# Delta rule and top-2 router on one core: keys used as they come, block copies laid out contiguously, joins and router pieces moved in the program

## The chip, the cores and the metric

One core of a Trainium2 chip runs the whole program in one launch. The metric is device time in microseconds (us), the median of the runs; lower is better.

## What is computed

For each of 4 x 8 batch-head pairs the delta rule walks 768 tokens with a 48 x 48 state. Its output, as 3072 tokens of 384 numbers, goes through a noisy top-2 router into 8 experts (384 to 1024 to 384).

```python
k_n = k / (np.linalg.norm(k, axis=-1, keepdims=True) + 1e-06)
for t in range(S):
    y[:, :, t] = np.einsum('bhd,bhde->bhe', q[:, :, t], state)
    v_old = np.einsum('bhde,bhd->bhe', state, kt)
    state = state + bt[:, :, :, None] * np.einsum('bhd,bhe->bhde', kt, vt - v_old)
# x: (B*S, H*D)
noisy_logits = x @ w_gate + np.log1p(np.exp(x @ w_noise)) * noise
# two largest per token, softmax over the two, then
out[token] += weight * (np.maximum(x @ w1[e], 0.0) @ w2[e])
```

## The kernel before, in words

The delta rule is done in 12 chunks of 64 tokens. A **unit** is one chunk of two batch entries: 128 partitions hold 2 x 64 tokens, the free axis 8 heads. A chunk has two units, and two chunks (four units) make a **step**; there are six steps. Everything is float32.

Per unit: `products` (L313) transposes the keys on TensorE (`turned`, L293, matmuls of L297, copied to `kT` on ScalarE), forms K K^T in `p_k` (L307), and copies its 32 x 32 blocks on ScalarE: the diagonal blocks to `gd` (L330, four copies of 32 partitions), the off-diagonal ones to `at` (L332, two copies of 32 partitions). Per step, `normalize` (L261) comes first: ScalarE squares the keys, VectorE sums them, a chain of small operations gives the inverse norm `ksc`, and GpSimd multiplies the keys by it (L287), so that every later use of the keys waits for that.

Per step, `invert` (L334) inverts the 32 x 32 triangles of all 128 (unit, head, block) cases at once on VectorE: a blockwise transposition of `gd` to `t` (L343), a product with `low_b`, 30 pairs of operations (L353, L357), a scaling, and two transpositions to `tt` (L369) and `tb` (L373). `join` (L377) copies `tt` into the 64 x 64 matrices `w64` on ScalarE (L387, four copies a unit), and fills their fourth quarter by two rounds of matmuls (L393, L402) with ScalarE copies between (L398, L407).

`recur` (L467) is the recurrence of a chunk in three stages: the state's part is subtracted from v (`p_b`, L307; VectorE L477), the rows are solved (`p_u`, L485; ScalarE copy `u`, L490), and the state is updated (`p_s`, L503; VectorE L510 or L512; GpSimd copies of it to `wide`, L515). `within` makes the masked products of queries and keys `qk` one chunk ahead, `answer` the outputs `y` and the router's logits one chunk behind. `route` (L518) handles the four tiles of a finished step on VectorE: top two, then the row of each token in its expert's list, by two matmuls into `p_at` (L583, L584), then eight GpSimd scatters to DRAM (`spread`, L170).

The program's loop hands out these pieces: `inverse`, `answers`, `nexts` are generators, and `take(work, n)` runs n pieces at the marked places. In an even chunk the inversion of the next step starts, and `normalize` and the route of the step before are there whole; the joins of the next step come at the end of an odd chunk. A scheduler then fixes one order per engine, which the engine follows strictly, so a waiting instruction holds all behind it. `gd`, `t`, `tt` and `tb` have one buffer each.

When all rows are scattered, the experts run one after the other on TensorE (L702, L709, L718), and a loop over the 24 tiles gathers and adds the two rows of each token (L783 to L798).

## Time and profile before

| | before |
|---|---|
| median of 3 runs | 1264.98 us (1264.11 to 1267.48) |
| the profiled execution, its own time | 1273.34 us |
| its span | 1271.6 us |
| TensorE matmul busy | 936.2 us (74%) |
| VectorE busy | 341.6 us (27%) |
| ScalarE busy | 332.5 us (26%) |
| GpSimd busy | 168.7 us (13%) |
| mean granted TensorE clock | 0.795 of full |

The shares are means over three stages that differ much: the delta rule and router (to about 588 us), the experts, and the last gather. A term is read from the timeline of its own stage. "issue" in a row is idle time before an instruction for which the profile shows no releaser.

### The profile page before, as it was taken

How to read it: one execution, taken by the hardware profiler on the slowest of the kernel's cores; microseconds unless marked ns; L12 is line 12 of the kernel's file. 1: busy time of each engine (PE TensorE's matmuls, PEld its weight loads, DVE VectorE, ACT ScalarE, POOL GpSimd, SP SyncE). 2: the span in 40 equal slices, each digit the busy share in tenths (PEclk: the TensorE clock that was granted, in tenths of full speed). 3: DMA queues.
4: the chain of work that ended last, by engine and by line, in shares of the span. 5: the costliest groups of instructions: out<-in, count | busy, mean ns of one | idle time of the engine just before them, and what ended most of it. 6: DMA issues, size and time to landing. Idle time of an engine off the chain costs nothing. (4 is left out here: it accounts for less than half of the span.)

```text
span 1271.6 us, 20241 instructions
## 1 busy us (share of the span) xinstructions
PE 936.2 (74%) x8634; PEld 628.1 (49%) x8634; DVE 341.6 (27%) x923; ACT 332.5 (26%) x693; POOL 168.7 (13%) x222
## 2 busy tenths in 40 slices
PE   2143756847648678834999999999999999999400
PEld 2133745736537567633565555555555555555200
DVE  2764382572753712121010010101101010110112
ACT  3474644554355233110202011020201102010021
POOL 5102113032131120220000000000000000000265
PEclk9555766657558655556999999999999999999755
DMA  5941292726622120116112231301213120100266
GB/s 105 343 144 19 54 324 74 209 83 186 228 64 40 27 63 3 51 44 236 52 42 93 75 112 62 124 34 54 100 74 112 62 81 0 38 7 23 86 199 186
DMA packets 142658, 124.31 MB, mean 98 GB/s; under 512 B 84704, under 2 KB 134880, under 8 KB 142560
## 3 DMA queue, kind: packets, MB, share of 16 engines
q1 hardware_dynamic: 135520, 103.95, 26.0%
q0 software_dynamic: 6144, 18.88, 4.7%
q8 instruction: 70, 1.15, 0.3%
q10 hardware_dynamic: 896, 0.10, 0.1%
q14 instruction: 28, 0.23, 0.1%
HBM read 59.99 MB, written 62.91 MB: 97 GB/s over the span
## 5 line engine op out<-in xcount | busy, mean ns | idle before, releaser
L709 PE MATMUL p_h<-xe,w1e 128*128 128x448 f32 x768 | 290.7, 540 | 1.5 <-DVE xe L703 1.5
L718 PE MATMUL p_o<-w2e,hT 128*128 128x384 f32 x896 | 290.3, 486 | 0.0
L718 PEld LDWEIGHTS p_o<-w2e,hT 128*128 128x128 f32 x896 | 170.2, 190 | 119.6 <-issue 3.0
L709 PEld LDWEIGHTS p_h<-xe,w1e 128*128 128x128 f32 x768 | 145.3, 190 | 142.9 <-issue 139.7
L713 ACT ACTIVATE hT<-p_h 128x448 f32<-128x448 f32 x128 | 69.6, 544 | 526.8 <-PE p_h L709 526.8
L722 DVE COPY yr<-p_o 128x384 f32<-128x384 f32 x56 | 31.2, 558 | 543.0 <-PE p_o L718 543.0
L783 POOL DMA_INDIRECT got<-rows_y,slot x48 | 46.9, 977 | 644.0 <-PEq L756 624.4
L297 PE MATMUL p_t<-ident,kp 128*128 128x128 f32 x96 | 22.6, 390 | 86.6 <-POOL kp L287 85.8
L353 DVE TENSOR_TENSOR part<-t 128x30 f32<-128x30 f32 (+9 forms) x180 | 64.1, 356 | 4.7
L357 DVE TENSOR_TENSOR t<-t,part 128x30 f32<-128x30 f32 (+9 forms) x180 | 63.8, 354 | 4.8
L330 ACT COPY gd<-p_k 32x256 f32<-32x256 f32 x96 | 56.3, 586 | 25.0 <-PE p_k L307 14.4
L387 ACT COPY w<-tt 32x256 f32<-32x256 f32 x96 | 60.1, 626 | 9.5 <-DVE tt L369 8.2
L297 PEld LDWEIGHTS p_t<-ident,kp 128*128 128x128 f32 x96 | 16.2, 203 | 88.6 <-POOL kp L287 86.8
L170 POOL DMA_INDIRECT rows_x<-y,slot x48 | 46.9, 976 | 85.9 <-issue 52.0
L515 POOL COPY wide<-st 64x384 f32<-64x384 f32 x44 | 26.3, 599 | 172.2 <-DVE st L512 136.2
L583 PE MATMUL p_at<-r_taken,mask_u 128*128 128x32 f32 x12 | 3.6, 396 | 54.4 <-DVE gate L531 22.7
L702 PE MATMUL p_xt<-ident,xr 128*128 128x128 f32 x168 | 21.7, 290 | 27.9 <-DMA xr<-rows_x 27.9
L503 PE MATMUL p_s<-u,kp 64*64 64x48 f32 x704 | 30.8, 284 | 15.2 <-issue 15.1
L440 PE MATMUL p_y<-u,qk 64*64 64x48 f32 x768 | 40.2, 274 | 0.0
L790 ACT ACTIVATE got<-got,gate 128x384 f32<-128x384 f32 x24 | 14.7, 614 | 97.2 <-DMA got<-rows_y,slot 91.1
L307 PE MATMUL p_b<-st,kT 64*64 64x48 f32 x704 | 31.2, 283 | 12.0 <-issue 11.9
L440 PEld LDWEIGHTS p_y<-u,qk 64*64 64x64 f32 x768 | 36.5, 189 | 4.5 <-issue 3.7
(119 smaller groups left out, 892.9 us busy)
## 6 DMA issues: line engine op xcount, KB each, us to landing
rows_y<-zero SPq DMA_DIRECT2D x8, 3264.0 KB
w1e<-in_moe_w_dram SPq DMA_DIRECT2D x8, 1536.0 KB
w2e<-in_moe_w_dram SPq DMA_DIRECT2D x8, 1536.0 KB
rows_x<-zero SPq DMA_DIRECT2D x8, 1344.0 KB
xr<-rows_x SPq DMA_DIRECT2D x8, 1344.0 KB
rows_y<-yr SPq DMA_DIRECT2D x56, 192.0 KB
kp<-in_k_dram SPq DMA_DIRECT2D x48, 96.0 KB
qp<-in_q_dram SPq DMA_DIRECT2D x48, 96.0 KB
```

The lines of the kernel that those rows point to most:

```text
L170: d = nc.gpsimd.indirect_dma_start(out=rows_x, out_offset=bass.IndirectOffsetOnAxis(ap=slot, axis=0), in_=rows, in_offset=None,).ins
L297: nc.tensor.transpose(p_t[:, j], src[:, 2 * j : 2 * j + 2], ident)
L307: nc.tensor.matmul(out[rows_of[b], z, j], lhsT[rows_of[z], j, rows_of[b]], rhs(rows_of[z], j, b), start=(j == 0), stop=(j == NP - 1), skip ...
L330: nc.scalar.copy(gd[rows], p_k[rows, :, :, n * Q : (n + 1) * Q])
L353: nc.vector.tensor_tensor(out=part, in0=t[:, j + 1 :, j, None].to_broadcast(shape), in1=t[:, None, j, 0:j].to_broadcast(shape), op=ALU.mult,)
L357: nc.vector.tensor_tensor(out=t[:, j + 1 :, 0:j], in0=t[:, j + 1 :, 0:j], in1=part, op=ALU.add)
L387: nc.scalar.copy(w64[rows, :, cols], tt[rows])
L440: nc.tensor.matmul(p_y[b, h], qk[b, h % 2, h // 2], u[b, h], start=(c == 0 and h == 0), stop=(h == H - 1), skip_group_check=True,)
L709: nc.tensor.matmul(p_h, w1e[:, do, fo * 128 : (fo + 1) * 128], xe[:, do, cols], start=(do == 0), stop=(do == KT - 1),)
L713: nc.scalar.activation(hT[:, fo, cols], p_h, ACTF.Relu)
L718: nc.tensor.matmul(p_o, hT[:, fo, i * 128 : (i + 1) * 128], w2e[:, fo], start=(fo == 0), stop=(fo == FT - 1),)
L783: nc.gpsimd.indirect_dma_start(out=g, out_offset=None, in_=rows_y, in_offset=bass.IndirectOffsetOnAxis(ap=slot[:, n : n + 1], axis=0),)
```

## The change

- `normalize` is gone: the keys stay as loaded. The squared norms are read from the diagonal of the transposed `gd` in `invert`, and the chain that gives the norm now stands there, on [128, 32] tiles, followed by d = beta / norm^2 and by `low_d`, a GpSimd product of 128 x 1024 numbers that the inversion's first product needs. `low_b`, which it replaces, depended on inputs alone.
- `norms`, transposed back, multiplies v on GpSimd: `scale(c)`, two products of 128 x 384 per chunk, as large as the products on keys that are gone.
- `gd` and `tt` are laid out [128, 32 heads, 32] instead of [128, 32, 32 heads], so that ScalarE's block copies read and write runs of 32; the VectorE transpositions of `gd` and to `tt` now have one strided side. `at` is copied once per unit with 128 partitions.
- At the start the joins of only two units come ahead of the loop. Later joins are given out in pieces, the first of them at the end of the odd chunk.
- `route` has yields, and is begun in the middle of the even chunk. Its running count is one reduction; the sum over earlier tiles goes to four matmuls with `ones` (there was one). Three small VectorE operations are fused away.
- On the load queue, the keys of step 2 now stand ahead of the eight clears of `rows_x`.

```diff
-        def normalize(s):
...
         def products(n):
...
-            for b in range(2):
-                for n in range(2):
-                    rows = slice(b * C + n * Q, b * C + (n + 1) * Q)
-                    nc.scalar.copy(gd[rows], p_k[rows, :, :, n * Q : (n + 1) * Q])
-                    if n == 0:
-                        nc.scalar.copy(at[rows], p_k[rows, :, :, Q:C])
+            nc.scalar.copy(at, p_k[:, :, :, Q:C])
+            for lo in range(0, 128, Q):
+                rows = slice(lo, lo + Q)
+                nc.scalar.copy(gd[rows], p_k[rows, :, :, lo % C : lo % C + Q])
 
         def invert(s):
...
+            nc.vector.transpose(
+                out=t, in_=step[s, "gd"].rearrange("p h i -> p i h"),
+            )
+            nc.vector.tensor_copy(ss, diagonal)
+            nc.vector.tensor_scalar_max(root, ss, 1e-30)
+            nc.scalar.activation(root, root, ACTF.Ln)
+            nc.scalar.activation(root, root, ACTF.Exp, scale=0.5)
+            yield
+            nc.vector.reciprocal(norm, root)
+            nc.vector.tensor_tensor(out=norm, in0=norm, in1=ss, op=ALU.mult)
+            nc.vector.tensor_tensor(out=norm, in0=norm, in1=root, op=ALU.add)
+            nc.vector.tensor_scalar(
+                out=norm, in0=norm, scalar1=0.5, scalar2=1e-6, op0=ALU.mult, op1=ALU.add
+            )
+            nc.vector.tensor_tensor(out=d, in0=norm, in1=norm, op=ALU.mult)
+            nc.vector.reciprocal(d, d)
+            nc.vector.tensor_tensor(out=d, in0=d, in1=beta_s, op=ALU.mult)
+            nc.gpsimd.tensor_tensor(
+                out=low_d, in0=low, in1=d[:, None, :].to_broadcast([128, Q, Q]), op=ALU.mult
+            )
+            nc.vector.transpose(out=norms, in_=norm)
+            yield
+            nc.vector.tensor_tensor(out=t, in0=t, in1=low_d, op=ALU.mult)
...
+            nc.vector.transpose(out=tt.rearrange("p h i -> p i h"), in_=scaled)
...
+        def scale(c):
+            for n in range(c * NU, (c + 1) * NU):
+                nc.gpsimd.tensor_tensor(
+                    out=v, in0=v,
+                    in1=step[s, "norms"][:, i * H : (i + 1) * H, None].to_broadcast(
+                        [128, H, D]
+                    ),
+                    op=ALU.mult,
+                )
...
         def route(s):
...
+            for i in range(1, US):
+                nc.tensor.matmul(
+                    p_at[:, i:], ones, taken[:, 0 : US - i],
+                    start=False, stop=False, skip_group_check=True,
+                )
+            nc.tensor.matmul(
+                p_at, ones, before[:, None, :].to_broadcast([128, US, E]),
+                start=False, stop=True,
+            )
...
         for c in range(NCH):
             s = c // 2
+            scale(c)
             if c % 2 == 0:
                 inverse = [invert(s + 1)] if s + 1 < NS else []
                 take(inverse, 1)
-                if s + 2 < NS:
-                    normalize(s + 2)
...
             for i, _ in enumerate(recur(c)):
                 if i == 0:
                     take(answers, 3)
                     if grams:
                         products(grams[0])
-                    take(inverse, 6)
+                    take(inverse, 9)
+                    take(joins, 2)
+                    take(routes, 3)
                 elif i == 1:
-                    take(answers, 3)
+                    take(answers, 4)
                     if grams:
                         products(grams[1])
-                    take(inverse, 6)
+                    if c % 2 == 0:
+                        take(inverse, 9)
+                        take(joins, 2)
+                        if c:
+                            routes = [route(s - 1)]
+                    else:
+                        take(inverse, 99)
+                    take(routes, 3)
```

How the instructions move, at three places. TensorE, where the first chunk's solve (`p_u`) stands, before: it follows the transposition of a key tile of step 2.

```order
L402 MATMUL p_x<-w_3_157,x 32x32 x16
L307 MATMUL p_q<-qT,kT 64x64 x16
L297 MATMUL p_t<-ident,qp_142 128x128 x4
L307 MATMUL p_q<-qT,kT 64x64 x16
L297 MATMUL p_t<-ident,kp_132 128x128 x4
L485 MATMUL p_u<-v,w_0_148 64x48 x7
```

The same place in the change:

```order
L384 MATMUL p_x<-w_0_148,x 32x32 x16
L384 MATMUL p_x<-w_1_151,x 32x32 x16
L267 MATMUL p_t<-ident,kp_132 128x128 x4
L375 MATMUL p_x<-tb,at 32x32 x16
L277 MATMUL p_k<-kT 64x64 x16
L375 MATMUL p_x<-tb,at 32x32 x2
L384 MATMUL p_x<-w_2_154,x 32x32 x16
L375 MATMUL p_x<-tb,at 32x32 x14
L480 MATMUL p_u<-v,w_0_148 64x48 x16
```

The solve now follows the joins of its own two units and parts of the other two; the key transposition ahead of it needs a load alone.

TensorE in a later step, before: the router's `p_at` stands behind the solve of the even chunk and ahead of its state update `p_s`.

```order
L485 MATMUL p_u<-v,w_3_157 64x48 x16
L451 MATMUL p_xt<-ident,y 128x128 x3
L459 MATMUL p_xt<-wgn,xT 128x16 x3
L583 MATMUL p_at<-r_taken,mask_u 128x32
L297 MATMUL p_t<-ident,kp_126 128x128 x4
L584 MATMUL p_at<-r_earlier,ones 128x32
L297 MATMUL p_t<-ident,qp_144 128x128
L307 MATMUL p_k<-kT 64x64 x16
L503 MATMUL p_s<-u,kp_132 64x48 x16
L503 MATMUL p_s<-u,kp_134 64x48 x16
```

In the change:

```order
L480 MATMUL p_u<-v,w_3_157 64x48 x16
L433 MATMUL p_xt<-ident,y 128x128 x3
L267 MATMUL p_t<-ident,kp_126 128x128 x4
L441 MATMUL p_xt<-wgn,xT 128x16 x3
L277 MATMUL p_k<-kT 64x64 x16
L498 MATMUL p_s<-u,kp_132 64x48 x16
L498 MATMUL p_s<-u,kp_134 64x48 x16
L267 MATMUL p_t<-ident,qp_144 128x128 x4
L267 MATMUL p_t<-ident,qp_146 128x128 x4
L277 MATMUL p_q<-qT,kT 64x64 x32
L277 MATMUL p_b<-st_2965,kT 64x48 x16
L277 MATMUL p_b<-st_2986,kT 64x48 x16
```

`p_at` follows these rows: it has moved behind the state update, the next queries and the next `p_b`.

VectorE at the turn of a step, in the change (before, a transposition of `gd` is followed by the product with `low_b` after one state update, and the two long transpositions to `tt` and `tb` stand half a step ahead):

```order
L350 TENSOR_TENSOR scaled<-t,d 128x1024
L355 STREAM_TRANSPOSE tt<-scaled 128x32x32
L356 STREAM_TRANSPOSE tb<-scaled 128x32x32
L507 TENSOR_TENSOR st_3375<-p_s,st_2965 128x384
L307 STREAM_TRANSPOSE t<-gd 128x1024
L507 TENSOR_TENSOR st_3396<-p_s,st_2986 128x384
L313 COPY ss<-t 128x32
L314 TENSOR_SCALAR root<-ss 128x32
L401 TENSOR_TENSOR qk<-p_q,mask 128x512
L318 RECIPROCAL norm<-root 128x32
L319 TENSOR_TENSOR norm<-norm,ss 128x32
```

The odd chunk's state update now stands directly behind the end of one inversion and around the start of the next.

## Rows read from the trace of the kernel before

**Rows 1.** Page, part 2: busy tenths and clock tenths, 31.8 us per digit.

```profile
PE   2143756847648678834999999999999999999400
...
PEclk9555766657558655556999999999999999999755
```

**Rows 2.** Timeline, 560 to 600 us: start us, us, engine, line, operation; idle before it.

```profile
571.01 0.96 POOL L170 DMA_INDIRECT rows_x<-y,slot  x1 [0.30 <-issue]
...
588.45 4.49 PE L702 MATMUL p_xt<-ident,xr 128*128 128x128 f32 x21 [27.93 <-DMA xr<-rows_x]
```

**Rows 3.** Groups by line: xcount | busy us, mean ns of one | idle before, releasers.

```profile
L297 PE MATMUL p_t<-ident,kp 128*128 128x128 f32 x96 | 22.6, 390 | 86.6 <-POOL kp L287 85.8 <-issue 0.8
...
L583 PE MATMUL p_at<-r_taken,mask_u 128*128 128x32 f32 x12 | 3.6, 396 | 54.4 <-DVE gate L531 22.7 <-DVE gate L601 22.5 <-DVE r_taken L531 9.2
```

**Rows 4.** Timeline, startup, 14 to 154 us.

```profile
14.48 0.94 ACT L270 ACTIVATE ksq<-kp 128x384 f32<-128x384 f32 x2
...
20.48 1.97 PE L297 MATMUL p_t<-ident,kp 128*128 128x128 f32 x8 [20.48 <-POOL kp L287]
...
36.03 0.58 ACT L330 COPY gd<-p_k 32x256 f32<-32x256 f32 x1
...
36.64 1.25 DVE L343 STREAM_TRANSPOSE t<-gd 128x1024 f32<-128x1024 f32 x1 [17.27 <-ACT gd L330]
...
54.25 2.06 PE L297 MATMUL p_t<-ident,kp 128*128 128x128 f32 x8 [22.42 <-POOL kp L287]
...
69.53 1.92 PE L393 MATMUL p_x<-tb,at 32*32 32x32 f32 x64 [3.78 <-DVE tb L373]
...
115.03 1.11 PE L297 MATMUL p_t<-ident,kp 128*128 128x128 f32 x4 [23.71 <-POOL kp L287]
...
116.08 0.98 PE L485 MATMUL p_u<-v,w 64*64 64x48 f32 x13
...
125.31 1.02 DVE L510 COPY st<-p_s 128x384 f32<-128x384 f32 x2 [11.30 <-PE p_s L503]
...
151.92 1.25 DVE L343 STREAM_TRANSPOSE t<-gd 128x1024 f32<-128x1024 f32 x1 [1.47 <-ACT gd L330]
```

**Rows 5.** Groups by line again: prices of ScalarE, GpSimd and VectorE operations.

```profile
L387 ACT COPY w<-tt 32x256 f32<-32x256 f32 x96 | 60.1, 626 | 9.5 <-DVE tt L369 8.2
...
L330 ACT COPY gd<-p_k 32x256 f32<-32x256 f32 x96 | 56.3, 586 | 25.0 <-PE p_k L307 14.4 <-remote 6.1 <-PE p_s L503 3.6
...
L332 ACT COPY at<-p_k 32x256 f32<-32x256 f32 x48 | 19.3, 401 | 0.0
...
L407 ACT COPY w<-p_x 32x256 f32<-32x256 f32 x48 | 17.4, 363 | 6.7 <-PE p_x L402 5.9
...
L338 POOL TENSOR_TENSOR low_b<-low,beta_b 128x1024 f32<-128x1024 f32 x6 | 14.1, 2357 | 28.3 <-DVE tb L373 11.2 <-DVE r_d L531 6.0 <-DVE r_a_hit L531 5.7
...
L373 DVE STREAM_TRANSPOSE tb<-scaled 128x1024 f32<-128x1024 f32 x6 | 12.0, 1993 | 0.0
...
L369 DVE STREAM_TRANSPOSE tt<-scaled 128x1024 f32<-128x1024 f32 x6 | 7.4, 1242 | 0.1
...
L278 DVE RECIPROCAL rec<-root 128x32 f32<-128x32 f32 x6 | 2.1, 347 | 1.1 <-ACT root L277 1.1
```

**Rows 6.** Timeline, one step, 253 to 288 us.

```profile
258.13 1.12 PE L297 MATMUL p_t<-ident,kp 128*128 128x128 f32 x4 [6.11 <-POOL kp L287]
...
264.08 0.86 ACT L490 COPY u<-p_u 128x384 f32<-128x384 f32 x2
...
278.70 0.61 PE L583 MATMUL p_at<-r_taken,mask_u 128*128 128x32 f32 x2 [11.38 <-DVE gate L531]
...
287.29 0.46 PE L503 MATMUL p_s<-u,kp 64*64 64x48 f32 x4 [0.95 <-issue]
```

**Rows 7.** Windows: us, busy of PE, PEld, DVE, ACT, POOL; granted clock; DMA share.

```profile
300.00:310.00 10.00, 7.36 (x185) 6.39 (x181) 1.11 (x2) 6.33 (x15) 0.00 (x0) 1.00 1.02 349
...
490.00:500.00 10.00, 10.00 (x132) 8.76 (x135) 0.00 (x0) 2.22 (x6) 0.00 (x0) 0.50 0.02 3
```

More of the change, by code (lines that the diff above doesn't have):

```diff
@@ L347, in invert @@
-            nc.vector.tensor_tensor(out=t, in0=t, in1=low_b, op=ALU.mult)
+                out=low_d, in0=low, in1=d[:, None, :].to_broadcast([128, Q, Q]), op=ALU.mult
+            )
+            norms = step[s, "norms"] = sb([128, UH], "norms", 2)
+            nc.vector.transpose(out=norms, in_=norm)
+            yield
+            nc.vector.tensor_tensor(out=t, in0=t, in1=low_d, op=ALU.mult)
             for j in range(1, Q - 1):
@@ L573, in route @@
             top1, hit1 = take_largest(rest, "b")
+            p1, den = gates[1][:, to], gates[0][:, to]
+            vv(p1, top1, top0, ALU.subtract)
+            nc.scalar.activation(p1, p1, ACTF.Exp)
             taken, at = full("taken"), full("at")
             vv(taken, hit0, hit1, ALU.add)
-            earlier = full("earlier")
-            for i in range(US):
-                nc.vector.tensor_copy(earlier[:, i], before)
-                vv(before, before, taken[:, i], ALU.add)
             p_at = bank([128, US, E], "p_at")
             nc.tensor.matmul(p_at, mask_u, taken, start=True, stop=False)
-            nc.tensor.matmul(p_at, ones, earlier, start=False, stop=True)
+            for i in range(1, US):
[6 more added lines that the diff above has]
+                start=False, stop=True,
+            )
+            yield
+            count = sb([128, E], "r_count", 1)
+            nc.vector.tensor_reduce(
+                out=count, in_=taken.rearrange("p u e -> p e u"), axis=AX.X, op=ALU.add
+            )
             vv(at, p_at, part[:, None, :].to_broadcast([128, US, E]), ALU.add)
+            vv(before, before, count, ALU.add)
             for hit, slot in ((hit0, slots[0]), (hit1, slots[1])):
@@ L608, in take, with now @@
                     work.pop(0)
+        def now(*work):
+            take(list(work), 999)
         nc.scalar.preload_act_table_set("natural_log_exp_and_others")
@@ L618, in deltanet @@
         load_router()
+        for n in range(2 * US, 3 * US):
+            load(n, "k")
         for e in range(E):
             cleared.append(clear(rows_x, e * N, e * N + TILES * 128))
-        for n in range(2 * US, 3 * US):
-            load(n, "k")
         first_weights = load_weights(w_even, 0)
-        def now(work):
-            for _ in work:
-                pass
-        normalize(0)
         for n in range(US):
@@ L632, in deltanet @@
         now(invert(0))
-        normalize(1)
         for n in range(US, 2 * US):
             products(n)
-        for n in range(US):
-            now(join(n))
         for n in range(NU):
             now(within(n))
-        def route_later(s):
-            route(s)
-            yield
-        inverse = []
+        for n in range(NU):
+            now(join(n))
+        inverse, joins, routes = [], [join(n) for n in range(NU, US)], []
         for c in range(NCH):
             s = c // 2
+            scale(c)
             if c % 2 == 0:
@@ L658, in deltanet @@
             nexts = [within(n) for n in range((c + 1) * NU, (c + 2) * NU) if n < NCH * NU]
-            joins = [join(n) for n in range((s + 1) * US, (s + 2) * US) if n < NS * US]
             for i, _ in enumerate(recur(c)):
@@ L679, in deltanet @@
                                 load(n, "k")
-        now(answer(NU * NCH - 2))
-        now(answer(NU * NCH - 1))
-        route(NS - 1)
+        now(*(answer(n) for n in range((NCH - 1) * NU, NCH * NU)))
+        now(route(NS - 1))
         return first_weights
```

96 lines of the change are left out of this document (33 added, 63 removed).

## The prediction, made before the change was run

> **What bounds the kernel now.** I read the page's slices first [rows 1]. In each slice the reader is to see which engine is full: TensorE stands between 1 and 8 tenths in the first 18 slices and at 9 from then to near the end. The kernel is thus two programs in a row: a delta rule with a router, in which no engine is full, and a dense stretch of experts. The border is sharp in the timeline [rows 2]: the last scatter of tokens starts at 571.01 us, the first expert matmul at 588.45, when the gathered rows have landed. From there on nothing is changed, so what the change is worth is how much earlier 588.45 comes.
>
> Second, the groups with their idle time [rows 3]. Two of them say what TensorE waits for in the first stage: 85.8 us for the keys that GpSimd has multiplied by their inverse norms, and 54.4 us for the router's counts, at `p_at`. Third, the timeline, to see where these waits lie and what is queued behind them. At the start [rows 4] the key transposition of 115.03 waited 23.71 us, and directly behind it stands the first solve, 116.08; the first state is there at 125.31. In a later step [rows 6] the transposition of 258.13 waited 6.11 us with the even chunk's solve behind it, and `p_at` of 278.70 waited 11.38 us with the state update behind it. Both are on the recurrence. I take them at full length, and look for what comes late next.
>
> **Term 1, the start.** Before, ScalarE's first piece of work is a square at 14.48, the transposition of keys starts at 20.48, ScalarE's last block copy at 36.03, and the first VectorE transposition at 36.64 [rows 4]. Now the keys need no norm. Per unit ScalarE has one copy to `kT` (0.59, as the wider copies of this trace) and five block copies. The block copies to `gd` and `w64` took 586 and 626 ns; those of the same size with both sides in runs took 401 (`at`) and 363 (`w64` from `p_x`) [rows 5]. The new ones lie between 363 and 626; I take 400, because the shape is that of `at`, and the same for the `at` copy over 128 partitions. Four units are 4 x (0.59 + 5 x 0.40) = 10.4 us, with about 1 us of matmuls ahead: the transposition of `gd` comes at about 26 in place of 36.64.
>
> The inversion gets longer. The transpositions of `gd` and to `tt` get a strided side; between 1.24 us (`tt` now) and 1.99 us (`tb`, strided on both) [rows 5] I take 1.99, which adds 1.5. The norm chain adds some nine small VectorE operations at 0.19 to 0.35, two on ScalarE and their handovers, an estimate of 3.4 us from the 347 ns of a reciprocal [rows 5] and the normalization's own like operations. `low_d` is 2.36 us on GpSimd, by `low_b`, and no longer ahead of time; at the start two products on v stand ahead of it, 1.8. Against this, the norms of step 1 no longer interrupt the first inversion (four sums and seven small operations, about 3.6). From 26, the 32.9 us from transposition to first join matmul (36.64 to 69.53) [rows 4] plus 1.5 + 3.4 + 4.2 - 3.6 give about 64; I say 66, for a queue of v products on GpSimd.
>
> Then the gain. Before, the first solve came 46.6 us after the first join, because all four joins and the key transposition of step 2 stood ahead, and those keys' norms stood behind the second inversion on VectorE. Now two joins and parts of two more stand ahead: two rounds of ScalarE copies and matmuls, about 11 us. The solve is at 77, the state some 10.5 later (9.2 before), at 87.5 in place of 125.31. The next chunk I let take as long as before: third transposition 26.6 us after the first state, 151.92. In the change the transpositions to `tt` and `tb`, 4 us, stand in that place on VectorE. So 118 in place of 152: **34 us**. Bounds: 20 (the joins' queue costs what the keys' did for one unit more) and 42.
>
> Of the other startup waits for keys, 20.48 is in this term, and the 22.42 at 54.25 [rows 4] cost nothing, since VectorE was in the inversion until about 69.
>
> **Term 2, keys in the later steps.** 85.8 less 20.48, 22.42 and 23.71 leaves 19.1 us in three waits. The next transposition needs only a load that was issued a step ahead; the solve behind it needs v and `w64`, which were there several us before. **19 us**; bounds 10 (something else late) and 19. GpSimd's products on v replace those on keys one for one and are needed a chunk later, so I price them at nothing; the cover is the rest of the chunk, and without it four products at 0.9 us a step would show.
>
> **Term 3, the route.** Of the 54.4 us, the sixth wait, about 5.5, lies behind the recurrence and stays. For the others `p_at` now stands behind the state update, the queries and `p_b`, some 6 us of TensorE work. VectorE, though, mixes route and inversion one for one: behind the state update I count in its order some 14 inversion operations, 15 of the route and four long ones ahead of the counts, about 11 us. So about 5 us of each wait stay; the first route, which stands whole behind the second loop inversion, keeps all. Gains of 6, 6, 4 and 1 make **17 us**; bounds 0 and 43. The three extra matmuls with `ones`, at the 0.4 of a `p_at` matmul [rows 3], are paid for by the eight small VectorE copies and sums between the two matmuls that go. The scatters stay eight a step, and with them a stretch in which TensorE goes on in bursts with 0.95 us of idle time, released by nothing that the profile shows [rows 6]; I gain and lose nothing there.
>
> **Term 4, ScalarE's queue.** In each chunk with new keys the copies to `u`, 264.08 in [rows 6], wait behind six block copies of 4 x 0.59 + 2 x 0.40 = 3.15 us, now 2.0. Eight chunks at 1.15: **9 us**, bounds 0 and 12. The shorter `w64` copies (16 a step) fall while TensorE is at other work: nothing.
>
> **Longer inversions in later steps** I price at nothing: `tb` was done about 40 us ahead of the joins that need it, and VectorE has to stay below the step's 84 us. If that cover goes, it is the rival below. Moving the keys ahead of the clears on the load queue shifts loads that were early: nothing.
>
> **Sum.** 34 + 19 + 17 + 9 = 79 us. The profiled execution took 1273.34 us with a span of 1271.6, 8.4 above the median of 1264.98; taken off the median, 79 gives **1186 us** (and a span near 1193). Ends of the terms do not come all together; its own range is 1160 to 1212.
>
> **Rival 1, the waits move.** Behind the keys and the counts stands the chain itself, and p_b, solve and update have to meet VectorE between inversion operations. If the later steps stay as long as they are, only term 1 is left: 1265 - 34 = 1231. For it: five later steps are alike although their waits differ, and VectorE's order now puts both state updates against long operations. Against: nothing else in the later steps ended TensorE's waits for long.
>
> [...]
>
> **Rival 3, slower: the inversion becomes the bound.** Its chain is now transposition, norm, ScalarE, GpSimd's `low_d` behind the copies of the state, then 60 operations mixed with the route, and the two transpositions directly ahead of the joins. Per step that is 1.5 + 3.4 + 2.4, about 8 us with handovers, and the lead of 40 us is given up by the new order. If `tb` ends later than the odd chunk's state update in every step, five steps give 5 x 8 = 40 and the removed waits bring nothing, since TensorE waits at the joins; with 10.6 gained at the start and two startup inversions of 8 each lost, this is +45: 1310. It decides from the point where VectorE's step passes 84 us. Against: VectorE was busy 341.6 us in the whole run.
>
> **Rival 4, no effect**: the start is bound elsewhere (the loads) and all else is hidden: about 1262.
>
> **How the numbers follow.** Forecast 0.62, rival 1 0.16, rival 2 0.13, rival 3 0.06, rival 4 0.03. Over or under 0.3%, about 4 us, is what a measurement can tell here: faster 0.91, same 0.03, slower 0.06. The range from 1142 to 1233 takes in most of rivals 1 and 2 and leaves out rivals 3 and 4 and the far ends, some 0.15.
>
> **What would show it.** First `gd` transposition near 26, first state near 88, third transposition near 118, first expert matmul near 510; no wait of the key transposition for GpSimd; `p_at` waits near 5 us; block copies near 0.40. It is wrong if the step from transposition to transposition stays at 84 (rival 1), if the clock row shows long stretches of 9 ahead of the experts (rival 2), or if the join matmuls of L375 wait for `tb` in the later steps (rival 3).

## The result, and the profile after

The change takes 1202.05 us (median of 4 runs, 1196.75 to 1207.17), the kernel before beside it 1266.23 (4 runs, 1264.11 to 1281.67): a ratio of 0.9468, 95% interval 0.9382 to 0.9554, so 64 us less. The forecast was 1186, the range 1142 to 1233.

The profiled execution of the change took 1196.75 us with a span of 1195.0. Against the span of 1271.6 before, that is 76.3 us, 12 more than the medians show: the profile of before lies 7 above its median, that of after 5 below. Everything changed lies ahead of the first expert matmul, which comes at 511.37 in place of 588.45 [rows 2]: 77.1 us. The page's slices of the change, for [rows 1], 29.9 us a digit:

```profile
PE   3265678788676788089999999999999999999200
...
PEclk9657566757666665589999999999999999999655
```

TensorE is fuller (5 to 8 from the third slice to the sixteenth, where it was 3 to 8), and its granted clock is hardly higher: a mean of 0.64 up to the first expert matmul, where it was 0.63. The start, for [rows 4], from the timeline of the change, VectorE first (start, length, engine, line, operation, idle time before it):

```profile
24.80 1.90 DVE L307 STREAM_TRANSPOSE t<-gd 128x1024 f32<-128x1024 f32 x1 [18.52 <-ACT gd L300]
...
87.13 0.56 DVE L505 COPY st<-p_s 128x384 f32<-128x384 f32 x1 [4.53 <-PE p_s L498]
...
109.28 1.92 DVE L307 STREAM_TRANSPOSE t<-gd 128x1024 f32<-128x1024 f32 x1
```

The same view of TensorE, first join, first solve, and what comes about the second chunk:

```profile
63.59 1.92 PE L375 MATMUL p_x<-tb,at 32*32 32x32 f32 x64 [22.61 <-DVE tb L356]
...
78.45 1.94 PE L480 MATMUL p_u<-v,w 64*64 64x48 f32 x32
...
115.02 1.14 PE L277 MATMUL p_q<-qT,kT 64*64 64x64 f32 x32 [11.09 <-ACT qT L269]
...
144.18 1.09 PE L480 MATMUL p_u<-v,w 64*64 64x48 f32 x14
153.05 1.13 PE L277 MATMUL p_k<-kT 64*64 64x64 f32 x32 [7.79 <-ACT kT L269]
153.96 2.97 PE L480 MATMUL p_u<-v,w 64*64 64x48 f32 x50
```

And the first expert matmul, for [rows 2]:

```profile
511.37 4.72 PE L714 MATMUL p_xt<-ident,xr 128*128 128x128 f32 x21 [27.90 <-DMA xr<-rows_x]
```

The first transposition of `gd` comes at 24.80 (26 was said), the first solve at 78.45 (77), the first state at 87.13 (87.5), the third transposition at 109.28 (118). Then TensorE waits for ScalarE: 11.09 us for `qT` at 115.02, and 7.79 us for `kT` at 153.05, in the middle of the solve of chunk 2. The groups that answer to [rows 3] and [rows 5]:

```profile
L369 ACT COPY w<-tt 32x256 f32<-32x256 f32 x96 | 38.6, 402 | 31.2 <-DVE tt L355 29.8
L300 ACT COPY gd<-p_k 32x256 f32<-32x256 f32 x96 | 34.8, 362 | 0.9
...
L328 POOL TENSOR_TENSOR low_d<-low,d 128x1024 f32<-128x1024 f32 x6 | 14.1, 2347 | 26.9 <-DVE d L326 23.9 <-DMA kp<-in_k_dram 2.9
...
L355 DVE STREAM_TRANSPOSE tt<-scaled 128x1024 f32<-128x1024 f32 x6 | 11.5, 1921 | 0.1
...
L297 ACT COPY at<-p_k 128x256 f32<-128x256 f32 x24 | 8.9, 372 | 11.7 <-PE p_k L277 11.5
...
L582 PE MATMUL p_at<-r_taken,mask_u 128*128 128x32 f32 x12 | 3.4, 369 | 20.5 <-DVE r_taken L526 15.0 <-DVE gate L526 5.5
```

The wait for GpSimd's products on the keys is gone; that at `p_at` fell from 54.4 to 20.5 us; the block copies take 362 and 402 ns where they took 586 and 626; a VectorE transposition with one strided side takes 1.92 us. What TensorE waits for now, in the list of waits up to the first expert matmul (total us, times, longest):

```profile
PE p_q L277 <- ACT qT L269: 23.7, 10, 11.1
...
PE p_k L277 <- ACT kT L269: 21.5, 6, 7.9
PE p_b L277 <- DVE qk L401: 15.1, 5, 5.1
...
PE p_u L480 <- ACT y L427: 8.1, 3, 3.4
```

Before, the same four were 6.8, 8.4, none and none. So by the first pair of traces the start and the later steps came out close to the sum. From the first solve of chunk 0 the gain is 37.6 us (116.08 to 78.45), from that of chunk 2 31.6 (175.75 to 144.18), and the rest of the stage takes 367.2 us in place of 412.7, 45.5 less where terms 2 to 4 add up to 45. The experiments show that it was made up of other things than those terms.

### The profile page after: what moved, and what is told of

The parts are those of the page before. It is cut to its first block, busy times and chain, and to the rows that moved or that the text cites. A ratio compares the mean times of both kernels' runs of the same rounds, so it can differ in the third digit from the quotient of the medians.

```text
span 1195.0 us, 20175 instructions
## 1 busy us (share of the span) xinstructions
PE 926.0 (77%) x8670; PEld 624.2 (52%) x8670; DVE 325.7 (27%) x875; ACT 272.5 (23%) x645; POOL 170.7 (14%) x222
## 5 line engine op out<-in xcount | busy, mean ns | idle before, releaser
L344 DVE TENSOR_TENSOR t<-t,part 128x30 f32<-128x30 f32 (+9 forms) x180 | 60.6, 337 | 4.7
L480 PE MATMUL p_u<-v,w 64*64 64x48 f32 x768 | 42.3, 281 | 9.3 <-ACT y L427 8.1
L510 POOL COPY wide<-st 64x384 f32<-64x384 f32 x44 | 23.5, 535 | 161.8 <-DVE st L507 145.7
L480 PEld LDWEIGHTS p_u<-v,w 64*64 64x64 f32 x768 | 40.0, 200 | 12.6 <-issue 9.7
L369 ACT COPY w<-tt 32x256 f32<-32x256 f32 x96 | 38.6, 402 | 31.2 <-DVE tt L355 29.8
L422 PE MATMUL p_y<-u,qk 64*64 64x48 f32 x768 | 45.0, 295 | 0.8 <-issue 0.8
L422 PEld LDWEIGHTS p_y<-u,qk 64*64 64x64 f32 x768 | 41.0, 209 | 5.2 <-issue 5.0
L375 PE MATMUL p_x<-tb,at 32*32 32x32 f32 x768 | 23.4, 229 | 24.4 <-DVE tb L356 22.6
L277 PE MATMUL p_b<-st,kT 64*64 64x48 f32 x704 | 25.8, 269 | 18.9 <-DVE qk L401 15.1
L277 PE MATMUL p_k<-kT 64*64 64x64 f32 x768 | 21.4, 266 | 21.5 <-ACT kT L269 21.5
L277 PE MATMUL p_q<-qT,kT 64*64 64x64 f32 x768 | 17.6, 248 | 24.6 <-ACT qT L269 23.7
```

What stands on the lines that cost most here:

```text
L277: nc.tensor.matmul(out[rows_of[b], z, j], lhsT[rows_of[z], j, rows_of[b]], rhs(rows_of[z], j, b), start=(j == 0), stop=(j == NP - 1), skip ...
L344: nc.vector.tensor_tensor(out=t[:, j + 1 :, 0:j], in0=t[:, j + 1 :, 0:j], in1=part, op=ALU.add)
L369: nc.scalar.copy(w64[rows, :, cols], tt[rows])
L422: nc.tensor.matmul(p_y[b, h], qk[b, h % 2, h // 2], u[b, h], start=(c == 0 and h == 0), stop=(h == H - 1), skip_group_check=True,)
L480: nc.tensor.matmul(p_u[b, h], w64[b, h], r[b, h], start=(h == 0), stop=(h == H - 1), skip_group_check=True,)
```

## The experiments

Kernels of one set ran on one chip, beside runs of the kernel before. The ratio is the one to before in the same set. "Later steps" is the stretch from the first solve of chunk 2 to the first expert matmul, in the one profiled execution; the busy and idle time of TensorE and its clock come from the windows view of that stretch. Executions of one kernel lie up to 23 us apart, so a difference of traces below 10 us is weak, and the ratios decide. The traces of e, b and d lie 13, 8 and 4 us above the medians of their kernels, that of i 8 below. Kernels c and d have the order of before, and d its layouts too, but both keep the change's rewritten count of the router.

| kernel | ratio, 95% interval | chunk 2 solved at | later steps | busy | idle | clock |
|---|---|---|---|---|---|---|
| before, first trace | | 175.75 | 412.7 | 260.7 | 152.0 | 0.61 |
| change, first trace | 0.9468 (0.938 to 0.955) | 144.18 | 367.2 | 253.7 | 113.5 | 0.63 |
| e: before again | | 180.30 | 360.9 | 230.4 | 130.5 | 0.66 |
| f: layouts alone | 0.9781 (0.970 to 0.986) | 163.60 | 342.1 | 222.3 | 119.8 | 0.68 |
| d: keys alone | 0.9979 (0.995 to 1.001) | 153.21 | 381.6 | 248.0 | 133.7 | 0.63 |
| c: keys, layouts, old order | 0.9650 (0.960 to 0.970) | 142.93 | 353.6 | 232.0 | 121.6 | 0.67 |
| b: keys, new order | 0.9937 (0.990 to 0.997) | 150.82 | 379.5 | 265.4 | 114.2 | 0.61 |
| a: the change again | 0.9657 (0.961 to 0.971) | 140.88 | 348.1 | 249.8 | 98.3 | 0.64 |
| h: the change, scatters left out | 0.9660 (0.960 to 0.972) | 144.21 | 337.7 | 237.1 | 100.6 | 0.68 |
| i: `w64` copies on GpSimd | 0.9495 (0.944 to 0.955) | 141.44 | 324.8 | 237.3 | 87.5 | 0.67 |
| j: `low_d` undone | 0.9618 (0.956 to 0.968) | 141.50 | 338.3 | 239.1 | 99.1 | 0.67 |
| l: i and j together | 0.9484 (0.942 to 0.954) | 138.95 | 322.1 | 230.6 | 91.5 | 0.70 |

"Chunk 2 solved at" is the first matmul of 64. In the change, a, b, h and j the first 14 stand 8 to 14 us ahead of the other 50 (a: 140.88 and 150.68), in the others of the table less than 2 us (c: 142.93 and 144.60). Counted from the 50, the change gains 23.5 us up to there in the first pair and 31.3 from e to a, and 8 us more behind it than the table says.

### a and e: both kernels once more

No edit.

> The change itself, timed again beside the three kernels that undo parts of it, so that all are compared on one chip. Theory 1 (the sum of the prediction, with waits traded against waits): 1202, a ratio to before of 0.947. Theory 2 (the profiled execution of the change, 1196.75, was a lucky one and that of before, 1273.34, an unlucky one): also 1202, with single executions spread over 10 us or more, while border times of one trace against another are no better than that.

Measured: 1170.96 us (6 runs) against 1213.5 (23 runs). Both theories said 1202, and both missed: in this set the change is 31 us faster than in the first, the kernel before 53 us, and the gain is 42 us, not 64. What is different in the kernel before?

> The kernel before, profiled once more, since its median was 1266 beside the first runs of the change and 1213.5 beside the four kernels of the first set. Theory 1 (what differs is how TensorE gets on beside the scatters): if this execution is near 1213, its state updates p_s run without the gaps of 0.25 to 0.97 us that the first trace shows beside the scatters (15.1 us of such idle time at p_s, 11.9 at p_b), and the steps are some 8 us shorter each, while the start is as it was; if it is near 1265, the gaps are there. Theory 2 (the granted clock differs): the gaps are the same and the clock of the first 590 us is higher than the 0.54 to 0.70 of the first trace.

Measured: 1221.96 us in one run; the runs of before beside it have a median of 1209.09 (17 runs), so this execution is 13 us above it. The two groups of the first trace, state updates and state parts:

```profile
L307 PE MATMUL p_b<-st,kT 64*64 64x48 f32 x704 | 31.2, 283 | 12.0 <-issue 11.9
L503 PE MATMUL p_s<-u,kp 64*64 64x48 f32 x704 | 30.8, 284 | 15.2 <-issue 15.1
```

and of this one:

```profile
L307 PE MATMUL p_b<-st,kT 64*64 64x48 f32 x704 | 24.1, 271 | 1.8 <-issue 1.8
...
L503 PE MATMUL p_s<-u,kp 64*64 64x48 f32 x704 | 20.8, 288 | 0.0
```

The idle time released by nothing visible has gone from 27.0 to 1.8 us, and the busy time of the two groups is 17 us less. In the first trace it stands beside the eight scatters of the first five steps, between bursts of mostly four to six matmuls (with [rows 6]):

```profile
285.88 0.46 PE L503 MATMUL p_s<-u,kp 64*64 64x48 f32 x4 [0.27 <-issue]
...
288.71 0.47 PE L503 MATMUL p_s<-u,kp 64*64 64x48 f32 x5 [0.96 <-issue]
```

The start is alike (first solve 116.08 and 116.06), the later steps are 51.8 us shorter. Of these, 21.5 are idle time (152.0 to 130.5) and 30.3 busy time (260.7 to 230.4), at a clock of 0.66 in place of 0.61. Theory 1 holds for the gaps; how much of the busy time is theory 2's, one trace does not separate. The first trace of the change has 1.9 us of such gaps on TensorE beside scatters, since the work that stands there now is another; instead ScalarE's copies of `y` stood still there. Of the five waits in the row below, four (3.9 to 6.0 us) last until a step's scatters are over or nearly so, and three of these gave the 8.1 us at `p_u` above. The longest, 8.8 us, begins 6 us ahead of its step's first scatter, and the matmuls of its `p_y` end at 381.4, 1.5 us before it starts, so only its end can stand beside them. From ScalarE's list of waits in that trace ("remote" is a release that the profile gives to no engine):

```profile
ACT y L427 <- remote: 28.7, 5, 8.8
```

The traces of a, c and e have no such wait. In the later steps the first pair gains 45.5 us, on the other chips the same stretch gains 360.9 - 348.1 = 12.8. Up to the first expert matmul the two gains differ by 25 us (77.1 and 52.2), by the medians of the sets by 22 (64 and 42). So 22 to 33 us of the first gain belong to its set. The 25 us of gaps at `p_s` and `p_b`, which the change happened to get out of the way of, are about as much; that they are the whole of it is not shown. The records name chip 8 (sets with a and i), 14 (e to h) and 11 (l), and none for the first pair; all 61 runs of before in the four later sets lie between 1198 and 1229 us, the first four between 1264 and 1282. Whether the chip or the loading of the program decides is open; it wasn't tried.

### g and h: the scatters left out

```diff
                 for slot in slots:
-                    spread(ys[n], slot[:, n : n + 1])
+                    if s == NS - 1:
+                        spread(ys[n], slot[:, n : n + 1])
```

(in both kernels; `yield` ahead of it in the change)

> The kernel before without the eight scatters of each of the first five steps; those of the last step stay. It leaves out the scattering of 20 of the 24 tiles into the experts' rows. Theory 1 (gaps beside scatters cost some 9 us a step): where before is near 1265, 45 us less, 1220; where before is near 1213, within 6 us of it. Theory 2 (the scatters stand beside waits that stay): within 6 us in either case.

> The change without the same scatters, in the same way. Theory 1: where before is near 1265, 20 us less than the change's 1202, since ScalarE's copies of y stood 28.7 us beside the scatters in its first trace and TensorE waited 8 us for them at p_u; where before is near 1213, within 6 us of 1171. Theory 2: within 6 us in either case.

Measured: ratios to before of 1.0035 (0.9998 to 1.0073) and 0.966 (0.960 to 0.972; the change itself 0.9657), that is 1213.46 and 1166.26 us. Where there are no gaps, the scatters cost nothing that these runs can tell in either kernel. The price of the gaps in a set that has them was not measured by leaving scatters out, since none of the later sets had them.

### b, c, d and f: the parts taken apart

The layouts undone (b):

```diff
-                step[s, "gd"] = sb([128, UH, Q], "gd", 1)
-            gd = step[s, "gd"].rearrange("p (u j z) i -> p u z j i", u=US, z=2)[:, i]
+                step[s, "gd"] = sb([128, Q, UH], "gd", 1)
+            gd = step[s, "gd"].rearrange("p i (u j z) -> p u z j i", u=US, z=2)[:, i]
...
-            tt = step[s, "tt"] = sb([128, UH, Q], "tt", 1)
+            tt = step[s, "tt"] = sb([128, Q, UH], "tt", 1)
...
-            nc.vector.transpose(out=tt.rearrange("p h i -> p i h"), in_=scaled)
+            nc.vector.transpose(out=tt, in_=scaled)
```

> The change with one part undone: gd and tt are laid out with the 32 heads innermost again, so that ScalarE's block copies read or write with a stride and the VectorE transpositions have none. Theory 1 (term 4 and its part of the start): the copies to u wait 1.15 us longer in eight chunks, the first gd transposition comes 3 us later, the transpositions are 0.6 us shorter: 11 us slower than the change, about 1213. Theory 2 (ScalarE's queue has become what TensorE waits for, at qT and kT, 45 us of waits in the change, with 16 block copies ahead of some): each step pays 16 x 0.22 + 8 x 0.2 = 5 us, six steps 30 us: 1232. Theory 3 (those copies are hidden): 1202.

The order undone (c):

```diff
+        for n in range(US):
+            done(join(n))
         for n in range(NU):
-            now(within(n))
-        for n in range(NU):
-            now(join(n))
-
-        inverse, joins, routes = [], [join(n) for n in range(NU, US)], []
+            done(within(n))
...
+            if c % 2 == 0 and c:
+                answers.append(route_later(s - 1))
...
+                    take(inverse, 99 if c % 2 else 5)
+                    if c % 2:
+                        take(joins, 99)
```

> The change with its order undone: four joins ahead of the loop, the joins of a step together at the end of the odd chunk, the route whole in the even chunk; keys as they come, the layouts and the load queue as in the change. Theory 1 (the terms of the prediction add up): the terms of the keys, of ScalarE's queue and more than half of the start stay (19 + 9 + 20), those of the order go: about 1217, p_at waits near 50 us in all, and the bursts of p_s with 0.25 to 0.95 us of idle time beside the scatters are back. Theory 2 (the order carries nearly all, since without it the solve waits for the counts in place of the keys): 1245 to 1255. Theory 3 (the keys carry nearly all): 1205.

Both undone (d), so that the keys are left, and with them the loads' order, the single `at` copy and the router's rewritten count:

> The order and the layouts of the change both undone: only keys as they come (with the products on v, low_d and the norm chain), the single at copy and the keys ahead of the clears on the load queue are left. Theory 1: start 15, later keys 19, about 1230. Theory 2 (order carries nearly all): 1255 or, with the longer inversion ahead of the joins, slower than before. Theory 3 (keys carry nearly all): 1212.

And the layouts alone in the kernel before (f):

```diff
-                step[s, "gd"] = sb([128, Q, UH], "gd", 1)
+                step[s, "gd"] = sb([128, UH, Q], "gd", 1)
...
-            for b in range(2):
-                for n in range(2):
-                    rows = slice(b * C + n * Q, b * C + (n + 1) * Q)
-                    nc.scalar.copy(gd[rows], p_k[rows, :, :, n * Q : (n + 1) * Q])
-                    if n == 0:
-                        nc.scalar.copy(at[rows], p_k[rows, :, :, Q:C])
+            nc.scalar.copy(at, p_k[:, :, :, Q:C])
+            for lo in range(0, 128, Q):
+                rows = slice(lo, lo + Q)
+                nc.scalar.copy(gd[rows], p_k[rows, :, :, lo % C : lo % C + Q])
...
-            tt = step[s, "tt"] = sb([128, Q, UH], "tt", 1)
+            tt = step[s, "tt"] = sb([128, UH, Q], "tt", 1)
```

> The kernel before with one part of the change alone: gd and tt laid out with runs of 32, block copies and transpositions accordingly, at copied once per unit; keys normalized ahead as before, order as before. Theory 1 (the two first sets of runs: layout is worth 3.0 to 3.3 per cent with keys as they come, because all 16 + 16 block copies of a step lie on the path): ratio to before 0.965 to 0.970, which is the whole of the change. Theory 2 (the prediction: 9 us at u, 3 at the start, 2 for at): ratio 0.989. Theory 3 (with normalized keys the wait for the keys takes the place of what the copies save): 0.995 to 1.000.

Measured: b 1204.54, c 1176.18, d 1211.57 (before 1213.5, the change 1170.96); f 1188.11 (before 1209.09, and its runs from 1171.49 to 1193.19). The absolute times of the expectations are those of the first set; the ratios are compared.

- **Layouts**: 0.9979 to 0.9650 with the old order, 0.9937 to 0.9657 with the new: 3.3 and 2.8 per cent, 40 and 34 us (35 and 34 by the medians). Alone, f, 2.2 per cent, with an interval that reaches to 3. For b, theory 2 (30 us) is nearest. For f the ratio falls between theories 1 and 2; the trace pair gives 35.5 us (541.18 to 505.65), with e 13 us above its median. Of what the layouts take from the later steps about half is waiting: 12.1 of 28.1 us from d to c, 15.9 of 31.5 from b to a, 10.7 of 18.8 from e to f. The rest is busy time at a higher clock: 0.67 for 0.63, 0.64 for 0.61, 0.68 for 0.66.
- **Keys**: alone 0.9979, nothing that is sure. On top of the layouts, 0.9781 to 0.9650, some 16 us, by two sets on two chips with intervals of 0.5 and 0.8 per cent. They bring the start forward (27.1 us at chunk 2, e to d; 20.7, f to c) and give it back in the later steps: 20.7 us longer, e to d; 11.5, f to c. None of the three theories for d had that. Part of this stretch is the router's rewritten count, which c and d keep: its 36 added matmuls take 8.6 us in each, and the wait ahead of them is 7 us shorter (54.0 to 47.5 from e to d, 54.4 to 46.9 from f to c).
- **Order**: 0.9650 to 0.9657 and 0.9979 to 0.9937: nothing, and half a per cent. For c, theory 1's 1217 is a ratio of 0.961 to 1266 and within the interval, but by terms that did not hold, and the bursts that it wanted back are not there. Yet the order does what it says: from c to a, the idle time of the later steps falls from 121.6 to 98.3 us, above all at `p_at`. The same stretch's busy time rises from 232.0 to 249.8. The windows of c, first to the solve of chunk 2, then to the experts (stretch, length, busy time and count of TensorE, of its weight loads, VectorE, ScalarE, GpSimd; granted clock; DMA):

```profile
142.93:496.49 353.56, 232.01 (x5102) 206.35 (x5102) 156.30 (x500) 126.09 (x330) 90.38 (x107) 0.67 0.44 139
```

and of a:

```profile
140.88:488.95 348.07, 249.79 (x5103) 222.16 (x5102) 153.53 (x487) 124.34 (x330) 90.97 (x107) 0.64 0.45 142
```

The same 5102 matmuls take 18 us more at a mean clock of 0.64 than at 0.67. One kind of matmul shows it alone, and beside it the wait that went. The groups of c:

```profile
L422 PE MATMUL p_y<-u,qk 64*64 64x48 f32 x768 | 36.5, 256 | 0.2 <-issue 0.2
...
L582 PE MATMUL p_at<-r_taken,mask_u 128*128 128x32 f32 x12 | 3.6, 397 | 46.9 <-DVE r_taken L526 28.7 <-DVE gate L526 18.1
```

and of a:

```profile
L422 PE MATMUL p_y<-u,qk 64*64 64x48 f32 x768 | 44.8, 295 | 0.5 <-issue 0.5
...
L582 PE MATMUL p_at<-r_taken,mask_u 128*128 128x32 f32 x12 | 3.6, 388 | 20.8 <-DVE r_taken L526 15.3 <-DVE gate L526 5.5
```

26 us of waiting at `p_at` went, and in this pair three quarters of the idle time saved came back as slower matmuls: `p_y` alone went from 256 to 295 ns each. The direction holds beyond the pair: `p_y` takes 278 to 295 ns in the eight traces with the new order and 251 to 274 in the six with the old. The size does not: h and j, with a's order, have 237.1 and 239.1 us of busy time, so 5 to 18 of the 23 us came back. That less waiting lowers the clock is not shown either, since i and l, with still less of it, have 0.67 and 0.70, and the layouts took waiting away and went with a higher clock.

### i: the remaining block copies taken off ScalarE

```diff
-                nc.scalar.copy(w64[rows, :, cols], tt[rows])
+                nc.gpsimd.tensor_copy(w64[rows, :, cols], tt[rows])
```

> The change with the 16 copies of tt into w64 of each step on GpSimd in place of ScalarE. Theory 1 (ScalarE's block copies lie in full on the path, as the two layout comparisons say: 7 us less of them a step brought 35 to 41 us): 6.4 us a step leave ScalarE, so some 25 to 35 us less than the change, about 1140 where the change takes 1170, if GpSimd copies a block in 0.5 us and so has them ready in time. Theory 2 (the copies themselves are late, since the joins' matmuls need w64, and their place in the queue behind ScalarE's other work does not matter): the slower engine makes each join later by 16 x 0.2 = 3 us, and GpSimd holds up VectorE's two-input operations meanwhile, as 0.70 for 0.20 us shows in the first trace of the change: 10 to 25 us slower than the change.

Measured: 1154.44 us, ratio 0.9495 (0.944 to 0.955), 1.6 per cent or 20 us below the change in its later run; faster than both kernels. What TensorE waits for in a, from its list of waits up to 600 us:

```profile
PE p_q L277 <- ACT qT L269: 23.5, 10, 10.4
...
PE p_k L277 <- ACT kT L269: 20.3, 6, 7.9
```

and in i:

```profile
PE p_q L277 <- ACT qT L269: 14.9, 9, 8.5
...
PE p_k L277 <- ACT kT L269: 12.2, 5, 7.9
...
PE p_x L384 <- POOL low_d L328: 3.3, 1, 3.3
```

The waits for `qT` and `kT` fall by 16.7 us, without the copies themselves being quicker, by i's groups:

```profile
L369 POOL COPY w<-tt 32x256 f32<-32x256 f32 x96 | 37.9, 394 | 18.7 <-DVE tt L355 8.9 <-DMA rows_x<-y,slot 5.3
```

It was the place in ScalarE's queue that cost. Theory 1 holds, at 20 in place of 25 to 35 us. With the copies their wait for `tt` has left the queue, too. In the first trace of the change ScalarE waits 29.8 us for it in all (the group of L369 above), most of it during the first inversion. But the 7.79 us for `kT` at 153.05 stand behind such a wait and eight copies:

```profile
149.09 3.30 ACT L369 COPY w<-tt 32x256 f32<-32x256 f32 x8 [5.35 <-DVE tt L355]
152.41 0.59 ACT L269 COPY kT<-p_t 128x512 f32<-128x512 f32 x1
```

In a the same place costs 7.8 us, in i nothing, and chunk 3 is solved 9.8 us earlier in i (177.96 to 168.18). How much of the 20 us is this wait and how much the copies themselves, i does not separate.

### j, k, l: the inversion, the tail, and both

j puts the product with d back on VectorE (in l with i):

```diff
+            nc.vector.tensor_tensor(out=t, in0=t, in1=low, op=ALU.mult)
             yield
...
-            nc.gpsimd.tensor_tensor(
-                out=low_d, in0=low, in1=d[:, None, :].to_broadcast([128, Q, Q]), op=ALU.mult
-            )
...
-            nc.vector.tensor_tensor(out=t, in0=t, in1=low_d, op=ALU.mult)
+            nc.vector.tensor_tensor(
+                out=t, in0=t, in1=d[:, None, :].to_broadcast([128, Q, Q]), op=ALU.mult
+            )
```

> The change with low_d undone: VectorE multiplies t by low while ScalarE is at the norm's logarithm and exponential, and by d behind the norm chain, in place of a GpSimd product of 2.35 us that it waited for 2.5 to 3.1 us in each inversion. Theory 1 (what keys as they come gave back in the later steps, some 20 of the 32 us that they brought at the start, is the longer inversion): about 3 us less in each of the three startup inversions, and as much in each later step that waits for tb: 10 to 18 us less than the change, about 1155 where the change takes 1170. Theory 2 (only the startup waits for the inversion): 4 us less. Theory 3 (one more operation of 1.2 us on VectorE, which also serves the recurrence, costs what it saves): within 3 us.

k takes a route out of the last chunk:

```diff
-                        take(routes, 4)
+                        take(routes, 4 if s + 1 < NS else 99)
```

> The change with one thing in its order undone: the route of the last step but one runs whole at the end of the even chunk 10, not in pieces into chunk 11. Theory 1 (from the first solve of chunk 10 to the first expert matmul the change takes 80.3 us, the kernel with the old order 73.5, because that route's counts and scatters stand in the last chunk): 5 to 7 us less than the change. Theory 2 (the last chunk's answers and the last route set the end, whatever is done before): within 2 us.

> The change with both: the copies of tt into w64 on GpSimd, and the product with d on VectorE in place of GpSimd's low_d. Theory 1 (with the copies on GpSimd its queue matters: TensorE waited 3.3 us for a join behind low_d and 1.7 behind a product on v, so taking low_d off GpSimd now helps more than alone): a ratio of 0.940 to 0.946, some 5 to 10 us less than with the copies alone. Theory 2 (the inversion has time to spare in the later steps whatever its length, and what is left is the start's 3 us): 0.947 to 0.950.

Measured: j 1168.59 us, 0.9618 (0.956 to 0.968); k 1175.85, 0.9652 (0.959 to 0.971); l 1148.67, 0.9484 (0.942 to 0.954). k gains nothing by its ratio (theory 2), though its interval of 7 us to either side reaches to theory 1. j's interval holds theories 2 and 3 and no change at all; theory 1's 0.950 to 0.957 is at its edge. l is level with i (theory 2), with an interval that reaches into theory 1. So no run shows that the keys' gain of the start went into `low_d` and its handover; the norm chain itself was not tried.

## Why the prediction was right, and where it was right by chance

The time lay in the range, 16 us above the forecast, and the trace's total was close: 77.1 us at the first expert matmul against a sum of 79, where the medians give 64. Term 1 was right in size. Term 4 was right as a mechanism and far too small. Terms 2 and 3, and the nothing for the gaps beside the scatters, were wrong. That these errors cancelled is luck.

- **Term 1, the start (34).** Right in size: the solve of chunk 2 starts 31.6 us earlier in the first pair, 39.4 on the other chips; by its last 50 matmuls 23.5 and 31.3. The mark by which the term was priced, the third transposition, came 42.6 us earlier (151.92 to 109.28), beyond the bound of 42, and the waits for `qT` and `kT` behind it gave some of that back. Beside the keys I named the joins, two ahead in place of four. From c to a they bring 4.4 us at the first solve (79.50 to 75.11), where the first trace of the change and h have 78.45 and 78.15; at chunk 2 they bring 2.0 by the first matmuls and lose 6.1 by the last 50. The keys that need no norm bring 27.1 at chunk 2, the layouts 16.7, both together 37.4.
- **Term 2, keys in the later steps (19).** Wrong. The waits went, as said, but "the solve behind it needs v and `w64`, which were there" did not hold for what stands around it: with keys alone the later steps have 133.7 us of idle time for 130.5, and 17.6 us more of busy time, of which 8.6 are the router's added matmuls and the rest goes with a lower clock. This is rival 1, for this term. What came late in the keys' place is ScalarE's copy `u`: in the later steps of d TensorE waits 20.9 us for it (9.7 in e), and 13.2 of these directly behind the solve of chunk 2, where e waits 1.1. There ScalarE waits for `tt`, copies six blocks of it, one to `at` and four to `gd`, and only then `u`. Of d, ScalarE and then TensorE:

```profile
162.83 3.81 ACT L370 COPY w<-tt 32x256 f32<-32x256 f32 x6 [8.93 <-DVE tt L355]
...
169.29 0.86 ACT L486 COPY u<-p_u 128x384 f32<-128x384 f32 x2
```

```profile
169.82 0.90 PE L434 MATMUL p_xt<-ident,y 128*128 128x128 f32 x3 [13.16 <-ACT u L486]
```

  At this one place the recurrence, 27 us ahead of e's, meets the end of an inversion. The rest of what d loses on e, up to chunk 8, is spread over small pieces that the traces do not tell apart.
- **Term 3, the route (17, bounds 0 and 43).** As a wait it was mis-sized the other way: 34 us less in the first pair, 26 from c to a. As time it was nothing. What failed, as far as the traces show it, is that the sum has nothing for the clock: from c to a the same matmuls ran slower, at a mean clock of 0.64 in place of 0.67. With the order it fell, with the layouts it rose (0.63 to 0.67 from d to c, 0.61 to 0.64 from b to a). The sign of rival 2, long stretches of 9 in the clock row ahead of the experts, did not show.
- **Term 4, ScalarE's queue (9, bounds 0 and 12).** The largest error. The layouts are worth 34 to 40 us by the ratios of b, c, d and a, 26 by f's. I counted only what stands ahead of `u` in chunks with new keys, and said of the 16 copies to `w64` in a step that they "fall while TensorE is at other work: nothing". A step has 16 copies to `gd` and 16 to `w64`; at 224 ns less each that is 7.2 us of ScalarE's time a step, and the trace pair d and c gains 4.7 us at the first solve and 36 at that of chunk 8 (391.90 to 355.94), about 8 us a step while there are keys and joins, and 2 us from there to the end (38.4 at the border). So the whole stage gets shorter by about what the copies do. The copies stand ahead of `qT`, `kT`, `u` and `y` in one queue that runs in order (at 162.83 in d, six of them and five more copies ahead of the `u` for which TensorE waits 13.16 us), and i shows the same from the other side. But only about half of the gain in the later steps is waiting; the other half is less busy time at a higher clock (0.63 to 0.67 from d to c), and what ties that to the copies is open.
- **The gaps beside the scatters.** "I gain and lose nothing there" was wrong in the first pair, where 22 to 33 us belong to the set and the gaps themselves come to 25, and right on the other chips.

So in a set with gaps the change gains 64 us by the medians, in those without 42. The sum of 79, made on a trace with gaps, had neither the 22 to 33 of that set nor the 14 to 28 that the layouts bring beyond the 9 of term 4 and some 3 of term 1 (16 copies to `gd` at 0.19 each), and it had 19 and 17 for the keys and the route, which came to a loss and to nothing. Rivals 3 and 4 did not occur: TensorE waited for `tb` once, at the start (22.6 us). Of rival 3 the traces have one place, at chunk 2, where `tt` came late for ScalarE's copies. Rival 1's sign, a step that stays at 84 us, did not show: from the solve of chunk 2 to that of chunk 4 the first pair has 83.4 and 71.4 us. On the other chips that step was 74.3 before the change already, and is 66.6 in a.

The same `w64` block took 402 ns copied in runs of 32 and 626 with a stride, and I had said 400: it was the count on the path, not the price of one copy, that I had wrong.

## What to carry to other kernels

Before an in-order queue's copies are priced at nothing, take the whole of what it does per step and ask what each piece waits for and what stands behind it: here 7 us of ScalarE a step, spread over 32 small copies of which hardly one showed as a wait, were worth more than the two largest waits in the list. A wait in the list is an offer, not a gain; undo one part at a time on the chip, since parts that cancel look like a forecast that holds. And take idle time together with the clock: where the engine that was freed runs below its full clock (here at a mean of 0.64 ahead of the experts), look at busy time as well before the idle time is counted as won; here the mean clock moved with two parts of the change, and in opposite directions (0.67 to 0.64 with the order, 0.63 to 0.67 with the layouts).

## What the runs showed of the hardware

- The granted clock does not follow fullness here, as far as the profile's busy time shows it. In the first trace of the change TensorE has its full clock (1.00) in 5 us of which it is busy for 1.83, and half of it (0.50) in 10 us of which it is busy for 9.95. The windows of the first:

```profile
295.00:300.00 5.00, 1.83 (x96) 1.60 (x96) 5.00 (x15) 0.70 (x2) 4.33 (x6) 1.00 0.69 178
```

and of the second:

```profile
415.00:420.00 5.00, 5.00 (x108) 4.56 (x105) 0.55 (x1) 0.72 (x2) 0.00 (x0) 0.50 0.05 15
420.00:425.00 5.00, 4.95 (x55) 4.07 (x53) 0.00 (x0) 1.86 (x5) 0.00 (x0) 0.50 0.01 3
```

  In the trace of before it is the same [rows 7]. From c to a less waiting went with a lower mean clock (0.67 to 0.64), from d to c and from b to a with a higher one (0.63 to 0.67, 0.61 to 0.64). What makes the clock rise or fall in this stage the runs do not show.
- In the first pair's traces there are runs of gaps of up to 1.2 us on TensorE, and waits of up to 6.0 us on ScalarE, beside the GpSimd scatters. The later traces of the same programs have no such runs, only single stops without a visible releaser (up to 2.5 us in a). The kernel before took 1266 us in the set whose trace has the gaps and 1209 to 1215 in those whose traces have none.
- GpSimd copied a 32 x 256 block from SBUF to SBUF in 394 ns in i and 436 in l, about as fast as ScalarE (402).
